# Top-32 attention and a gated feed-forward on one core: one reciprocal for two tiles, low words in PSUM, another queue for the first queries, other slots for the last duos

## The chip, the cores and the metric

The kernel runs on one NeuronCore of one Trainium2 chip. Its engines work side by side, each through its own instructions in order, and meet at semaphores: TensorE (PE, matrix products), VectorE (DVE), ScalarE (ACT), GpSimd (POOL), and SyncE (SP), whose queue issues nearly all transfers. The metric is the device time of one execution in microseconds.

## The reference

The inputs are q, k and v of shape (8, 8, 576, 64) in fp32, and two weight matrices, which the kernel reads as pairs of 32-bit words and turns into fp32 itself.

```
scores = q k^T / sqrt(64)                                # per batch and head, 576 x 576
kth    = the 32nd largest score of each row
attn   = softmax over the scores >= kth (others -1e9), sum + 1e-9
x      = (attn v), heads side by side                    # 4608 x 512
h      = x w_in                                          # 4608 x 2048
out    = (h * clip(h + 3, 0, 6) / 6) w_out               # 4608 x 512
```

## The kernel before, in words

**Tiles.** Two heads form a *pair*, two pairs a *duo*. A duo handles one query tile of 128 rows for two pairs: u is 0 or 1 for the pair, t is 0 or 1 for the head within it. 576 is 4 x 128 + 64, so besides the four full query tiles there is a leftover tile of 64 rows per head; the two heads' leftover rows share one tile of 128 partitions, and such a *leftover duo* has one row tile per pair instead of two. There are 80 duos, 10 for each of 8 batches: 64 full ones and 16 leftover ones. In the last batch the two leftover duos come after query tile 0.

**Selection.** `scores` (PE, then ACT copies out of PSUM) makes the 576 scores of each row. `top` runs four rounds on DVE: MAX8 (L250) finds the eight largest, MATCH_REPLACE8 (L254) takes them out; after four rounds the 32nd largest is known. A full duo takes 16 of the first and 12 of the second.

**Softmax.** For each pair u: `shift` on POOL (L263, L266) forms a bias; `exp` on ACT masks by Prelu (L273), takes Exp with a running sum into `den` (L278), and adds EPS (L283); `inverse` on DVE is the reciprocal of `den` (L287); `weights` on POOL multiplies by it (L297) and splits the words into halves of 16 bits (L306, tile e); `flip` has a DMA of SP's queue transpose these (L312, tile t); `join` puts the halves together again (L318, tile eT), on ACT for u = 0 and on POOL for u = 1. `values` multiplies by v on PE (L338, tile pv), `place` copies the result on ACT into xT, or xr for leftover rows (L348).

**Feed-forward.** When both duos of a query tile are placed, 128 rows of x are complete and a block of feed-forward work is queued: 16 pieces, eight for h (L365, two pieces to one PSUM tile, of which ACT then takes a relu and a copy, L373 and L375, and POOL makes the *gate*, L379 and L380), eight for acc (L385, the product with w_out), at whose end ACT scales (L395) and SP stores (L397).

**Order.** Nothing is scheduled by a compiler: the order of instructions is the order of the program. Duo m owns slots 8m to 8m+7, one DVE round of one pair each. In each slot come, in this order: the round; the parts of any duo that are due there by a table (`usual`, `behind`, `early` for duos 0 and 1, `soon` for the last two); and pieces of feed-forward at a rate that follows how much is queued. In `usual` the second pair's shift stands at slot 8m+7, its Exp at 8m+8, the reciprocals at 8m+9 and 8m+13, the weights at 8m+10 and 8m+14, the transposes at 8m+12 and 8m+16, the joins at 8m+15 and 8m+19, values at 8m+22 (`behind`: 8m+25). The scores of duo m+1 stand at slot 8m+1. A slot is a place in the order, not a time: an engine that has not to wait runs ahead of it, another lags.

**Weights.** 32 chunks of weight words are loaded (st) and converted in the first 150 us, one step per slot: ACT takes the absolute value of the high words (L108, tile a) and scales the low words (L111, tile y); POOL clips a (L109); DVE shifts a (L117) and ORs the sign into y (L118); POOL adds both into the weight (L123). Both a and y come from `gpool` (8 buffers), which the gates' g tiles also use. PSUM has five banks for `ps_big` and three tiles (`ps_w`) for h, acc and pv.

**Start.** SP's queue loads the first pair's keys (three transfers), then its queries (three more), then weights and the other pairs. PE transposes keys and queries (L177), ACT copies them (L179 to L183), PE makes the first scores.

Of the kernel before, what the change touches and what calls it, by code (L numbers as in the profile page):

```python
# [9 lines left out]
ALU = mybir.AluOpType  # L10
F32 = mybir.dt.float32
U32 = mybir.dt.uint32
I32 = mybir.dt.int32
# [16 lines left out]
def kernel(  # L30
# [9 lines left out]
    nc = tc.nc  # L40
    P = nc.NUM_PARTITIONS
    B, H, S, D = q.shape
    DM, FF = moe_w_in.shape
    J = S // P
# [3 lines left out]
    NFC = FF // P  # L48
# [4 lines left out]
    def pool(name, bufs, **kw):  # L53
        return ctx.enter_context(tc.tile_pool(name=name, bufs=bufs, **kw))
# [8 lines left out]
    gpool = pool("g", 8)  # L63
# [3 lines left out]
    ps_w = pool("ps_w", 3, space=PSUM)  # L67
# [25 lines left out]

    WC = 512

    def convert(dst, src):

        st = kqpool.tile([P, 2 * WC], U32, tag="kq", name="st")
        nc.sync.dma_start(st[:], src)
        yield
        words = st[:].rearrange("p (n two) -> p n two", two=2)
        lo, hi = words[:, :, 0], words[:, :, 1]
        a = gpool.tile([P, WC], F32, tag="g", name="a")
        y = gpool.tile([P, WC], F32, tag="g", name="y")
        nc.scalar.activation(a[:], hi.bitcast(F32), AF.Abs)  # L108
        nc.gpsimd.tensor_scalar(a[:], a[:], HI_MOST, HI_LEAST, ALU.min, ALU.max)  # L109

        nc.scalar.activation(y[:], lo, AF.Copy, bias=2.0, scale=2.0**-51)  # L111
        yield

        au, yu = a[:].bitcast(U32), y[:].bitcast(U32)
        nc.vector.tensor_scalar(au, au, 3, None, ALU.logical_shift_left)  # L117
        nc.vector.scalar_tensor_tensor(  # L118
            out=yu, in0=hi, scalar=0x80000000, in1=yu,
            op0=ALU.bitwise_and, op1=ALU.bitwise_or,  # L120
        )
        yield
        nc.gpsimd.tensor_tensor(  # L123
            dst.bitcast(I32), a[:].bitcast(I32), y[:].bitcast(I32), ALU.add
        )

    def weight_chunks():
        win, wout = moe_w_in.bitcast(U32), moe_w_out.bitcast(U32)
        for f in range(0, FF, WC):
            for g in range(NHP):  # L130
                rows = slice(g * P, (g + 1) * P)
                yield w_in[:, g, f : f + WC], win[rows, 2 * f : 2 * (f + WC)]
        for c in range(NFC):
            rows = slice(c * P, (c + 1) * P)
            yield w_out[:, c, :], wout[rows, :]
# [3 lines left out]
    class Pair:  # L139
# [3 lines left out]
            self.b, self.hp = b, hp  # L143
            self.vm, self.vr, self.kr = vms[hp], vrs[hp], krs[b % 2 * NHP + hp]

        def load(self):
            h0 = 2 * self.hp
            t = self.landed = kqpool.tile([P, 2 * J + 1, 2, D], F32, tag="kq", name="landed")
            for i, src in enumerate((k, q)):
                for hh in range(2):  # L150
                    nc.sync.dma_start(
                        t[:, i * J : (i + 1) * J, hh, :],
                        src[self.b, h0 + hh, 0:JP, :].rearrange("(p j) d -> p j d", j=J),
                    )
                nc.sync.dma_start(
                    t[i * R : (i + 1) * R, 2 * J, :, :],
                    src[self.b, h0 : h0 + 2, JP:S, :].rearrange("h s d -> s h d"),
                )
# [26 lines left out]
    class Duo:  # L185
# [82 lines left out]
        def exp(self, u):  # L268

            nt, m = self.nt, self.m[u]  # L270
            for t in range(nt):
                row = self.row(u, t)
                nc.scalar.activation(  # L273
                    row, row, AF.Prelu, bias=m[:, t, TOP_K - 1 : TOP_K], scale=-1.0, alpha=FLAT
                )
            for t in range(nt):
                row = self.row(u, t)
                nc.scalar.activation(  # L278
                    row, row, AF.Exp, bias=self.less[u][:, t : t + 1], scale=-scale / FLAT,
                    accum_out=self.den[:, u, t : t + 1],  # L280
                )
            d = self.den[:, u, 0:nt]
            nc.scalar.activation(d, d, AF.Copy, bias=EPS)  # L283

        def inverse(self, u):
            d = self.den[:, u, 0 : self.nt]
            nc.vector.reciprocal(d, d)  # L287

        def weights(self, u):

# [35 lines left out]
        def values(self, dst):  # L326

            w = R if self.rest else P
            pv = ps_w.tile([P, 512], F32, tag="w", name="pv")
            for u in range(2):  # L330
                pr, eT = self.pairs[u], self.eT[u]
                for c in range(J + 1):
                    for hh in range(2):
                        if self.rest:
                            rhs = eT[:, c if c < J else J + hh, hh * R : (hh + 1) * R]
                        else:
                            rhs = eT[:, c if hh == 0 or c == J else J + 1 + c, :]
                        nc.tensor.matmul(  # L338
                            pv[hh * D : (hh + 1) * D, u * w : (u + 1) * w],
                            pr.vm[:, hh, c, :] if c < J else pr.vr[:, hh, :],  # L340
                            rhs,
                            start=(c == 0),
                            stop=(c == J),
                        )
            self.pv = dst, pv[:, 0 : 2 * w].rearrange("p (u q) -> p u q", u=2)

        def place(self):
            nc.scalar.copy(*self.pv)  # L348
# [55 lines left out]
    duos = []  # L404
    for b in range(B):
        halves = [pairs[b][0:2], pairs[b][2:4]]
        for qt in range(J):
            duos += [Duo(h, qt) for h in halves]


            if qt == (0 if b == B - 1 else J - 1) and not 2 < b < B - 1:
                duos += [Duo(h, J) for h in halves]
            elif 2 < b < B - 1 and qt % 2 == 0:
                duos.append(Duo(halves[qt // 2], J))
    assert J == NHP == 4
    per_batch = 2 * J + 2
    ND = len(duos)
# [65 lines left out]
    chunks = list(weight_chunks())  # L483
    landing, converting, adding = [], [], []

    def land(count=1):

        for _ in range(min(count, len(chunks))):
            c = convert(*chunks.pop(0))
            next(c)  # L490
            landing.append(c)

    def convert_step():


        for c in adding:
            next(c, None)
        adding.clear()
        if len(converting) >= 2 or not landing:
            for c in converting[:1]:  # L500
                next(c)
            adding.extend(converting[:1])
            del converting[:1]
        if landing:
            c = landing.pop(0)
            next(c)
            converting.append(c)
        land()

    def pair_at(m, first):  # L510
# [2 lines left out]
        return pairs[b + 1][at - first] if b + 1 < B and 0 <= at - first < NHP else None  # L513

    first = pairs[0]
    first[0].load()
    land(2)
    first[1].load()
    first[0].transpose()
# [5 lines left out]
    first[1].transpose()  # L525
    duos[0].scores((1,))
    land()

    usual = dict(
        shift0=3, exp0=4, inverse0=9, weights0=10, flip0=12, join0=15,
        shift1=7, exp1=8, inverse1=13, weights1=14, flip1=16, join1=19, values=22, place=23,
    )

    behind = dict(usual, values=25, place=26)
    early = dict(
        shift0=3, exp0=3, inverse0=4, weights0=4, flip0=5, join0=8,
        shift1=7, exp1=7, inverse1=8, weights1=8, flip1=9, join1=12, values=12, place=13,  # L540
    )
    soon = dict(
        shift0=3, exp0=3, inverse0=5, weights0=5, flip0=7, join0=10,
        shift1=7, exp1=7, inverse1=9, weights1=9, flip1=11, join1=14, values=16, place=17,
    )
    queued = {}
    for m in range(ND):
        for part, at in (early if m < 2 else soon if m >= ND - 2 else behind if per_batch <= m < ND - 4 else usual).items():
            queued.setdefault(8 * m + at, []).append((m, part))

    def parts(slot, late=None):

        for m, part in sorted(queued.get(slot, []), key=lambda x: x[1][:-1] != "shift"):
            if late is not None and (part[:-1] in ("inverse", "weights")) != late:
                continue
            if part == "values":
                values(m)
            elif part == "place":
                place(m)
            else:  # L560
                getattr(duos[m], part[:-1])(int(part[-1]))

    due = 0.0
    for m in range(ND + 3):
        u = duos[m] if m < ND else None
        for i in range(8):
            if u:
                u.top(i // 4, i % 4)
            if m < 4:
                parts(8 * m + i, False)  # L570
# [7 lines left out]
            if m < 4:  # L578
                parts(8 * m + i, True)
            else:  # L580
                parts(8 * m + i)
# [54 lines left out]
```

## Time and profile before

| | us |
|---|---|
| median of 5 runs | 1581.66 (1581.34 to 1582.38) |
| the profiled execution | 1582.23 |
| its span in the trace | 1580.4 |
| DVE busy | 1466.7 |
| PE busy | 1460.1 |
| POOL busy | 1143.1 |
| ACT busy | 1095.3 |
| mean granted TensorE clock | 0.961 of full |

DVE and PE are both busy over nine tenths of the span, but not at the same time: the trace shows DVE at work from 11.1 us, in its first selection round at 13.48 us, and at the end of its last at 1492.5 us; PE ends at 1576.7 us. Rows of the timeline give the start and the duration of an instruction (or of several in a row), then engine, line, operation, tile written and tiles read, and in brackets how long the engine stood idle before and what released it. Instructions of one engine overlap by a little, so that what one costs is read from the starts of its neighbours. Waits are listed as: who waited for whom, total, times, longest.

### The profile page before, as it was taken

What the parts mean: (1) busy time and instruction counts of PE and PEld (TensorE: products, weight loads), DVE (VectorE), ACT (ScalarE), POOL (GpSimd) and SP (SyncE); (2) the same over time, 40 slices, a digit from 0 to 9 for tenths busy, and PEclk for the clock granted to TensorE, in tenths of its full rate; (3) what the DMA queues carried; (4) which work ended last, traced back from release to release, by engine and by line L of the source; (5) the groups of instructions that cost most, each with busy time, mean ns of one, the idle gap of its engine ahead of it and who ended that gap; (6) DMA issues with size and microseconds to landing.
All of it is one profiled execution on the core that took longest, in us unless ns stands there. A gap on an engine that the chain in (4) does not pass through costs nothing.

```text
span 1580.4 us, 28787 instructions
## 1 busy us (share of the span) xinstructions
PE 1460.1 (92%) x10272; PEld 1041.7 (66%) x10272; DVE 1466.7 (93%) x3105; ACT 1095.3 (69%) x1865; POOL 1143.1 (72%) x1264
## 2 busy tenths in 40 slices
PE   5256799879999999998999999999999999999899
PEld 3152666567767777676777777776777767677675
DVE  6999999999999999999999999999999999999700
ACT  6675777677776777777776786777766787777521
POOL 4868687777867777767687777777687777767831
PEclk9667899989999999999999999999999999999999
DMA  8652544444444543545244443446344543533400
GB/s 236 159 181 44 114 83 87 88 91 97 79 91 88 97 83 77 104 85 118 57 99 82 99 88 75 93 98 117 56 91 86 100 85 75 105 63 68 83 22 14
DMA packets 450319, 144.49 MB, mean 91 GB/s; under 512 B 433280, under 2 KB 441472, under 8 KB 450176
## 3 DMA queue, kind: packets, MB, share of 16 engines
q1 hardware_dynamic: 450176, 142.65, 43.2%
q8 instruction: 81, 1.33, 0.3%
q14 instruction: 62, 0.51, 0.1%
HBM read 45.09 MB, written 9.44 MB: 35 GB/s over the span
## 4 chain that ended last, share of the span: by engine, by line
DVE 46%; PE 39%; POOL 7%; ACT 3%; issue 3%; DMA 1%; SPq 0%; POOLq 0%; ACTq 0%; DVEq 0%
DVE m L250 24%; DVE wk L254 21%; PE h L365 15%; PE acc L385 14%; PE pv L338 4%; PE big L232 3%; POOL e L306 2%; POOL sc L297 1%; POOL a L109 1%; ACT sc L278 1%; POOL eT L318 1%; ACT eT L318 1%; PE big L177 1%; PE big L215 1%; PE big L226 1%
## 5 line engine op out<-in xcount | busy, mean ns | idle before, releaser
L250 DVE MAX8 m<-wk 128x8 f32<-128x576 f32 x864 | 613.6, 747 | 2.2
L385 PE MATMUL acc<-w_out,g 128*128 128x512 f32 x1152 | 517.8, 601 | 13.6 <-POOL g L380 13.6
L365 PE MATMUL h<-xT,w_in 128*128 128x128 f32 x4096 | 485.9, 279 | 17.3 <-ACT xT L348 17.3
L365 PEld LDWEIGHTS h<-xT,w_in 128*128 128x128 f32 x4096 | 475.4, 195 | 39.6 <-issue 17.9
L254 DVE MATCH_REPLACE8 wk<-m,wk 128x576 f32<-128x576 f32 x576 | 424.0, 743 | 0.0
L385 PEld LDWEIGHTS acc<-w_out,g 128*128 128x128 f32 x1152 | 213.8, 192 | 260.5 <-issue 239.2
L297 POOL TENSOR_SCALAR sc<-sc,den 128x576 f32<-128x576 f32 x288 | 213.2, 750 | 220.9 <-DVE den L287 214.6
L306 POOL COPY e<-sc 128x2304 uint16<-128x2304 uint16 (+1 forms) x192 | 320.0, 1676 | 10.1
L278 ACT ACTIVATE sc<-sc,shift 128x576 f32<-128x576 f32 x288 | 220.3, 769 | 35.3 <-POOL shift L266 32.3
L318 ACT COPY eT<-t 128x2304 uint16<-128x2304 uint16 (+1 forms) x82 | 215.9, 2632 | 36.5 <-DMA t<-e 35.6
L273 ACT ACTIVATE sc<-sc,m 128x576 f32<-128x576 f32 x288 | 209.9, 776 | 40.6 <-DVE m L250 40.4
L338 PE MATMUL pv<-eT,vm 128*64 128x128 f32 (+1 forms) x2560 | 165.0, 274 | 56.2 <-ACT eT L318 45.7
L254 DVE MATCH_REPLACE8 wk<-m,sc 128x576 f32<-128x576 f32 x288 | 212.0, 743 | 0.0
L318 POOL COPY eT<-t 128x2304 uint16<-128x2304 uint16 (+1 forms) x78 | 203.7, 2611 | 7.0 <-DMA t<-e 6.6
L338 PEld LDWEIGHTS pv<-eT,vm 128*64 128x64 f32 x2560 | 136.0, 142 | 107.6 <-ACT eT L318 49.3
L250 DVE MAX8 m<-sc 128x8 f32<-128x576 f32 x288 | 203.5, 744 | 2.0 <-ACT sc L236 2.0
L373 ACT ACTIVATE g<-h,three 128x512 f32<-128x512 f32 x144 | 98.3, 683 | 154.4 <-PE h L365 145.1
L380 POOL TENSOR_TENSOR g<-g,hs 128x512 f32<-128x512 f32 x144 | 184.9, 1284 | 12.2 <-POOL g L379 0.2
L379 POOL TENSOR_SCALAR g<-g 128x512 f32<-128x512 f32 x144 | 89.0, 618 | 75.7 <-ACT g L373 66.1
L233 ACT COPY sc<-big 128x2048 f32<-128x2048 f32 (+1 forms) x65 | 119.2, 1834 | 27.5 <-PE big L232 27.3
L232 PE MATMUL big<-kq 64*128 64x512 f32 x512 | 136.0, 651 | 0.0
L395 ACT ACTIVATE o<-acc 128x512 f32<-128x512 f32 x36 | 21.4, 595 | 111.1 <-PE acc L385 111.1
(47 smaller groups left out, 1115.6 us busy)
## 6 DMA issues: line engine op xcount, KB each, us to landing
landed<-in_k_dram SPq DMA_DIRECT2D x64, 128.0 KB, 2.8
landed<-in_q_dram SPq DMA_DIRECT2D x64, 128.0 KB, 2.9
st<-in_moe_w_in_dram SPq DMA_DIRECT2D x16, 512.0 KB, 4.9
vm<-in_v_dram SPq DMA_DIRECT2D x64, 128.0 KB, 2.3
st<-in_moe_w_out_dram SPq DMA_DIRECT2D x16, 512.0 KB, 6.2
out_dram<-o SPq DMA_DIRECT2D x32, 256.0 KB, 2.4
t<-e SPq DMA_TRANSPOSE x160, 4.6
landed<-in_k_dram SPq DMA_DIRECT2D x32, 32.0 KB, 2.6
```

The costliest lines, as they stand in the source:

```text
L232: nc.tensor.matmul(banks[:, 2 * i + hh, :], pr.qT[d, qs], pr.kT[d, :])
L250: nc.vector.max(self.m[u][:, t, 8 * r : 8 * r + 8], self.cur[t])
L254: nc.vector.match_replace(wk, self.m[u][:, t, 8 * r : 8 * r + 8], self.cur[t], LOWEST)
L273: nc.scalar.activation(row, row, AF.Prelu, bias=m[:, t, TOP_K - 1 : TOP_K], scale=-1.0, alpha=FLAT)
L278: nc.scalar.activation(row, row, AF.Exp, bias=self.less[u][:, t : t + 1], scale=-scale / FLAT, accum_out=self.den[:, u, t : t + 1],)
L297: nc.gpsimd.tensor_scalar(row, row, self.den[:, u, t : t + 1], 1.0, ALU.mult, ALU.mult)
L306: nc.gpsimd.tensor_copy(halves[:, :, to : to + c1 - c0], words)
L318: copy(eT[:, 0 : self.nb, :] .rearrange("p c q -> p (c q)") .bitcast(U16) .rearrange("p (x h) -> p h x", h=2), self.t16[u][:, 0 : 2 * self ...
L338: nc.tensor.matmul(pv[hh * D : (hh + 1) * D, u * w : (u + 1) * w], pr.vm[:, hh, c, :] if c < J else pr.vr[:, hh, :], rhs, start=(c == 0), ...
L365: nc.tensor.matmul(h[:, (f - f0) * P : (f - f0 + 1) * P], w_in[:, i, f * P : (f + 1) * P], xT[:, i, :], start=(i == 0), stop=(i == NHP - 1),)
L380: nc.gpsimd.tensor_tensor(g[:], g[:], hs[:], ALU.mult)
L385: nc.tensor.matmul(acc[:], gs[f // nf][:, f % nf * P : (f % nf + 1) * P], w_out[:, f, :], start=(f == 0), stop=(f == NFC - 1),)
```

## The change

It has four parts.

1. **One reciprocal per duo.** `exp` no longer adds EPS; a new step `settle` does it for one pair or for both, and `inverse` takes the reciprocal for one pair or both. In `usual` both pairs' `settle` stands at slot 8m+8 and one reciprocal at 8m+13. The first pair's weights move from 8m+10 to 8m+13, its transpose from 8m+12 to 8m+15, its join from 8m+15 to 8m+18 (the second pair's transpose and weights stay at 8m+16 and 8m+14, its join at 8m+19). `early` and the new table `last` keep one reciprocal per pair.
2. **Low words in PSUM.** For the first 16 chunks (`early`) ACT writes the scaled low words into a PSUM tile of `ps_w`, and DVE's OR writes its result into a tile of `gpool` taken at that time. The other 16 chunks are as before.
3. **First queries by ACT's queue.** The three transfers of the first pair's queries are issued by ACT instead of SP.
4. **The last duos.** The leftover duos of the last batch come after query tile 1 instead of 0. `soon` now holds for duos 74 to 78, with one reciprocal at 8m+10 and values at 8m+18; duo 79 has `last`, with values at 8m+11; `behind` now ends at duo 71 instead of 75, and duos 72 and 73 have `usual`.

```diff
-    def convert(dst, src):
+    def convert(dst, src, early):
...
-        y = gpool.tile([P, WC], F32, tag="g", name="y")
+        y = (
+            ps_w.tile([P, WC], F32, tag="w", name="yp")
+            if early
+            else gpool.tile([P, WC], F32, tag="g", name="y")
+        )
...
+        ys = gpool.tile([P, WC], F32, tag="g", name="ys") if early else y
...
         nc.vector.scalar_tensor_tensor(
-            out=yu, in0=hi, scalar=0x80000000, in1=yu,
+            out=ys[:].bitcast(U32), in0=hi, scalar=0x80000000, in1=yu,
             op0=ALU.bitwise_and, op1=ALU.bitwise_or,
         )
...
         nc.gpsimd.tensor_tensor(
-            dst.bitcast(I32), a[:].bitcast(I32), y[:].bitcast(I32), ALU.add
+            dst.bitcast(I32), a[:].bitcast(I32), ys[:].bitcast(I32), ALU.add
         )
...
-        def load(self):
+        def load(self, queue=None):
...
-            for i, src in enumerate((k, q)):
+            for i, (src, eng) in enumerate(((k, nc.sync), (q, queue or nc.sync))):
...
-            d = self.den[:, u, 0:nt]
+
+        def inverse(self, us):
+
+            d = self.den[:, us[0] : us[-1] + 1, 0 : self.nt]
+            nc.vector.reciprocal(d, d)
+
+        def settle(self, us):
+            d = self.den[:, us[0] : us[-1] + 1, 0 : self.nt]
             nc.scalar.activation(d, d, AF.Copy, bias=EPS)
-
-        def inverse(self, u):
-            d = self.den[:, u, 0 : self.nt]
-            nc.vector.reciprocal(d, d)
...
-            if qt == (0 if b == B - 1 else J - 1) and not 2 < b < B - 1:
+            if qt == (1 if b == B - 1 else J - 1) and not 2 < b < B - 1:
...
-            c = convert(*chunks.pop(0))
+            c = convert(*chunks.pop(0), early=len(chunks) >= NFC)
...
-    first[0].load()
+    first[0].load(nc.scalar)
...
     usual = dict(
-        shift0=3, exp0=4, inverse0=9, weights0=10, flip0=12, join0=15,
-        shift1=7, exp1=8, inverse1=13, weights1=14, flip1=16, join1=19, values=22, place=23,
+        shift0=3, exp0=4, shift1=7, exp1=8, settle01=8, inverse01=13, weights0=13, weights1=14,
+        flip0=15, flip1=16, join0=18, join1=19, values=22, place=23,
     )
...
     soon = dict(
-        shift0=3, exp0=3, inverse0=5, weights0=5, flip0=7, join0=10,
-        shift1=7, exp1=7, inverse1=9, weights1=9, flip1=11, join1=14, values=16, place=17,
+        shift0=3, exp0=4, shift1=7, exp1=8, settle01=8, inverse01=10, weights0=10, weights1=11,
+        flip0=12, flip1=13, join0=15, join1=16, values=18, place=18,
+    )
+    last = dict(
+        shift0=3, exp0=3, settle0=3, inverse0=5, weights0=5, flip0=7, join0=10,
+        shift1=7, exp1=7, settle1=7, inverse1=8, weights1=8, flip1=9, join1=11, values=11, place=11,
     )
...
-        for part, at in (early if m < 2 else soon if m >= ND - 2 else behind if per_batch <= m < ND - 4 else usual).items():
+        if m < 2:
+            when = early
+        elif m == ND - 1:
+            when = last
+        elif m >= ND - 6:
+            when = soon
+        else:
+            when = behind if per_batch <= m < ND - 8 else usual
+        for part, at in when.items():
```

## The prediction

> **What bounds the kernel now.** I read the page's busy times and slices first, then the waits of DVE and PE, then the timeline at three places: the start, the weight conversion, and the end.
>
> ```profile
> PE 1460.1 (92%) x10272; PEld 1041.7 (66%) x10272; DVE 1466.7 (93%) x3105; ACT 1095.3 (69%) x1865; POOL 1143.1 (72%) x1264
> ...
> PE   5256799879999999998999999999999999999899
> ...
> DVE  6999999999999999999999999999999999999700
> ```
>
> DVE is full from the first to the third-last slice, then stops; PE is thin in the first eight slices and full to the end. So DVE's top-32 rounds set the pace, and PE, which got its work late, drains what is left.
>
> ```profile
> DVE a L117 <- POOL a L109: 13.6, 2, 10.3
> DVE den L287 <- ACT den L283: 10.6, 6, 6.7
> DVE m L250 <- ACT sc L236: 2.0, 2, 1.3
> ```
>
> These are all of DVE's waits but a 0.8 us one for PEq at the start. The 6.7 comes after its last round. In the loop little is left to remove but its instructions.
>
> ```profile
> PE h L365 <- ACT xT L348: 6.0, 2, 3.4
> PE pv L338 <- POOL eT L318: 4.6, 2, 4.4
> PE big L226 <- ACT kr L183: 2.3, 1, 2.3
> ```
>
> PE's waits from 600 us on: it runs out of feed-forward work (h waits for xT) for the last time at 1087 us. Up to there a faster DVE brings PE's work forward one for one; after it PE is never short, and what is gained later counts only through the chain of the last duos. That chain is here:
>
> ```profile
> 1491.87 1.44 ACT L273 ACTIVATE sc<-sc,m 128x576 f32<-128x576 f32 x2 [3.96 <-DVE m L250]
> 1494.12 2.74 POOL L318 COPY eT<-t 128x2304 uint16<-128x2304 uint16 x1
> 1496.91 1.98 PE L338 MATMUL pv<-eT,vm 128*64 128x128 f32 x16 [4.40 <-POOL eT L318]
> 1514.56 1.09 PE L338 MATMUL pv<-eT,vm 128*64 128x128 f32 x16
> 1520.44 14.45 PE L365 MATMUL h<-xT,w_in 128*128 128x128 f32 x128
> ```
>
> DVE's last round ends at 1492.49. PE stands 4.4 us for duo 78's second eT, takes 1.98 where the same group takes 1.09 elsewhere (granted clock 0.75 in 1490 to 1500), and needs until 1576.67: 84.2 us after DVE.
>
> **The change part by part.**
>
> *Reciprocals.* 160 become 83: duos 0, 1 and 79 keep two, 77 save one.
>
> ```profile
> 1484.82 0.74 DVE L254 MATCH_REPLACE8 wk<-m,sc 128x576 f32<-128x576 f32 x1
> ...
> 1485.47 1.41 DVE L250 MAX8 m<-wk 128x8 f32<-128x576 f32 x2
> ...
> 1487.59 0.74 DVE L254 MATCH_REPLACE8 wk<-m,wk 128x576 f32<-128x576 f32 x1
> 1488.25 0.15 DVE L287 RECIPROCAL den<-den 128x2 f32<-128x2 f32 x1
> 1488.32 1.40 DVE L250 MAX8 m<-wk 128x8 f32<-128x576 f32 x2
> ```
>
> The row says 155 ns, but instructions overlap: replace to MAX8 is 0.65 without and 0.73 with it; the chain of waits books 0.07. So 77 x 0.07 = 5.4 us (6.2 at 0.08), not 11.9. Four elements instead of two cost nothing: 128x1 and 128x2 rows both lie in 142 to 167 ns. The EPS step (0.20 us on ACT) also goes 77 times, on an engine 69% busy: nothing.
>
> What moves: POOL's weights of tile 0 go from slot 10 to 13, so both tiles stand on POOL back to back behind one reciprocal: 1.47 + 2.10, twice, 7.1 us instead of 3.6. Behind them in POOL's order are the gates and the next duo's second shift, due 4.9 us after the reciprocal. The idle that POOL has today between the second reciprocal and that shift is mostly 0.5 us, so the shift slips by 3.0 to 3.6 us in almost every duo, and ACT's Exp with it. In its favour, the join of tile 0 (2.8 us, sometimes waiting for its transpose) leaves its place ahead of that Exp in ACT's order for one behind it. The reciprocal comes 14.5 us after the shift's due time in a full duo: covered. PE's cover is three PSUM tiles; its h groups today find the tile of two groups before free by 0.7 us at least, of three before by far more. SP issues the same transposes, one slot apart; outputs and loads behind them are not due for slots. I take +1 us (end: +22, below).
>
> *Low words in PSUM.* The OR of the first 16 chunks reads one input from PSUM and no second one from SBUF.
>
> ```profile
> 71.93 1.79 DVE L117 TENSOR_SCALAR a<-a 128x512 uint32<-128x512 uint32 x1
> 73.64 1.75 DVE L118 SCALAR_TENSOR_TENSOR y<-st,y 128x512 uint32<-128x512 uint32 x1
> ...
> 81.09 0.41 DVE L117 TENSOR_SCALAR a<-a 128x512 uint32<-128x512 uint32 x1
> 81.42 0.68 DVE L118 SCALAR_TENSOR_TENSOR y<-st,y 128x512 uint32<-128x512 uint32 x1
> ```
>
> It takes 0.68 alone and 1.09 or 1.75 beside POOL's work on the same tiles; over the first 16 chunks 4.5 us above 0.68. No row shows DVE reading PSUM. Ends: ACT's PSUM copy of the same size, 0.58, would give 6.0; if nothing is freed, 0. I take 2.9: the unheld row for most, some holding coming back at L117, which keeps its 5.3 us of excess. [...] PSUM has three tiles for this; chunk s needs chunk s-3's OR done, which today is so 3 us or more before. The second tile that the change takes from the g pool is taken later than today's, so ACT waits for g buffers no longer than now.
>
> *First queries on ACT's queue.* Three issues on SP, 2.82 to 4.77, go; ACT issues them before its table load (1.28 us, then about 2.7 to 4.0, with the first copy at 7.90).
>
> ```profile
> 6.53 0.93 PEld L177 LDWEIGHTS big<-ident,landed 128*128 128x128 f32 x5 [1.39 <-DMA landed<-in_q_dram]
> ...
> 7.90 1.01 ACT L179 COPY kq<-big 128x1024 f32<-128x1024 f32 x1 [5.90 <-PE big L177]
> ...
> 13.48 1.42 DVE L250 MAX8 m<-sc 128x8 f32<-128x576 f32 x2 [1.32 <-ACT sc L236]
> ```
>
> The chain from the queries to DVE's first round is unbroken, so what they land earlier, DVE starts earlier: 2.1 us at most (the issue times), nothing if the transfers share the engines. DMA share is 0.54 to 0.74 there, so most fits: 1.5. [...]
>
> *A gap that goes along.* At 133.7 DVE idles 3.30 us for POOL's clip; ACT waits 9.12 us for a g tile behind weights of tile 0 (125.62). Those weights now stand two rounds later. 0 to 3.3; I take 2.2.
>
> *Last six duos.* Pv 78 and 79 stand at slots 642 and 643, after the leftover block's h; in PE's order 20 matmuls of acc (8.6 us) and two blocks (56.1) follow, where 8 (3.6) and two blocks follow today. PE, never short, would reach pv 79 at today's 1576.7, less 10.5 (the gains below, by 1087), less 7.0 (today's standing at 1492 and the slow clock after it), less 67.0 (pv, acc, two blocks): 1492.2, which is E+11.7 if E is DVE's unstalled end in the sum below. But ACT's relu of the leftover block's first h, ready 18.2 us of PE work earlier (E-6.5), stands before duo 79's first Exp: with 1.2 + 3.5 its den comes at E-1.8, 3.0 late for the reciprocal (two slots before the end), so DVE ends at E+3.0. Then POOL in its order: gate, shift (to E+4.2), join 78 (2.8); ACT's Exp to 7.9; weights 3.6 (to 11.8), two gates (3.8); the transpose, 4.6, lands at 16.4, join to 19.2. Then half a pv 1.2, acc 8.6, blocks 56.1: E+85.1, and 1.5 for the clock, which also today follows PE's idling. So 86.6 against 84.2: the shorter chains gain nothing, because more is put behind them. Ends: 78.7 without the stall, 89 if two more gates (3.8) slip in ahead.
>
> **Sum.** 1492.5 - 5.4 - 2.9 - 1.5 - 2.2 = 1480.5 (E); + 86.6 + 1.0 = 1568.1; + 3.7 from the last matmul to the span's end as today = 1571.8; + 1.8 outside the span (1582.23 against 1580.4) = 1573.6. The profiled execution lies 0.57 above the median, so **1573**.
>
> **Rivals.**
> *The burst on POOL reaches DVE (slower).* Eight duos next to a leftover duo have their second den ready less than 3.6 us before the reciprocal (8, 18, 28, 41, 46, 61, 66, 72); slipped by their 3.0 to 3.6 they give 22.4 us of new waits: 1573 + 21 = 1594. For: four of them stand at 0.03 us now. Against: at 61 and 72 ACT, not POOL, was late, with the join before the Exp, which is moved. It decides from 12 us on.
> *PE hides it.* PE is 92% busy; if its last starvation isn't DVE's doing, little of DVE's gain arrives and the tail gives back 2.4: 1580 to 1582. Against: h waits for xT at 317, 730 and 1087.
> *The tail is free.* If the relu doesn't hold duo 79, 78.7 instead of 86.6: 1565. For: PE's lag behind its slot is a difference of large numbers.
> *Start and low words do nothing:* 1573 + 4.4 = 1577.4, inside the forecast's own range.
>
> **How the numbers follow.** Forecast 0.62 (own range 1567 to 1578), tail free 0.14, hidden 0.09, slower 0.15. The range 1563 to 1582 holds all but the slower case and a thin end. A measurement here tells 0.2% (3.2 us) from nothing: faster 0.76, same 0.09, slower 0.15.
>
> **What would show it.** 83 reciprocals; OR rows of the first 16 chunks near 0.7 us throughout; first MAX8 near 12.0; no idle at 133; DVE's last round near 1483.5, and PE's end 84 after it, with PE idle before duo 79's second half. Wrong if DVE den waits rise above 10 us inside the loop, or PE waits for PSUM tiles or gates.

## The result: slower by 3.3 us

| | before | after |
|---|---|---|
| median, us | 1581.17 (1579.76 to 1582.47, 48 runs) | 1584.45 (1581.86 to 1587.03, 28 runs) |
| ratio, 95% interval | | 1.002 (1.0015 to 1.0026) |
| profiled execution, us | 1582.23 | 1583.52 |
| end of DVE's last round, us | 1492.49 | 1490.54 |
| end of PE, us | 1576.65 | 1577.90 |
| DVE's waits for den inside the loop, us | 3.47 | 13.30 |

1573 was predicted, within 1563 to 1582; the result lies outside, on the slow side. The two profiled executions differ by 1.3 us, less than the medians; the changed kernel's runs spread more widely (5.2 us against 2.7). A ratio, here and below, is the time over that of the kernel before on the same chip; the interval reaches 0.9 us to either side here, and 1.3 to 2.2 us in the experiments.

### The profile after

Line numbers from here on are those of the changed kernel. The page's busy times and slices:

```profile
PE 1458.8 (92%) x10272; PEld 1039.8 (66%) x10272; DVE 1458.3 (92%) x3028; ACT 1079.9 (68%) x1788; POOL 1134.4 (72%) x1264
...
PE   5266898889999999998999999999999999999989
...
DVE  6999999999999999999999999999999999989600
```

DVE has 77 instructions fewer and is busy 8.4 us less (1466.7 before), yet it ends only 2 us sooner. The one slice of PE below 9 near the end was the third-last before and is the second-last now. DVE's waits (who for whom, total, times, longest) show what took its gain:

```profile
DVE den L293 <- ACT den L297: 19.5, 8, 5.6
DVE a L123 <- POOL a L114: 9.9, 1, 9.9
DVE m L257 <- ACT sc L243: 1.7, 1, 1.7
```

The wait for POOL's clip at 133.7 us is gone (13.6 in two waits before, now one), and the waits for den have nearly doubled, 10.6 to 19.5. One of them, 5.6, lies after the last round and holds nothing up; 0.63 lies at the start; 13.3 are in the loop.

PE's waits from 600 us on:

```profile
PE pv L348 <- POOL eT L328: 6.7, 1, 6.7
PE h L375 <- ACT xT L358: 5.0, 2, 3.7
PE big L233 <- ACT kr L190: 3.4, 1, 3.4
PE pv L348 <- ACT eT L328: 2.7, 2, 1.5
```

One stand of 6.7 us has taken the place of the 4.4 before. The timeline of all engines at the end shows where:

```profile
1492.88 1.43 ACT L280 ACTIVATE sc<-sc,m 128x576 f32<-128x576 f32 x2
...
1501.59 1.09 PE L348 MATMUL pv<-eT,vm 128*64 128x128 f32 x16 [1.23 <-ACT eT L328]
...
1506.80 2.73 POOL L328 COPY eT<-t 128x2304 uint16<-128x2304 uint16 x1 [2.18 <-DMA t<-e]
...
1509.59 1.97 PE L348 MATMUL pv<-eT,vm 128*64 128x128 f32 x16 [6.69 <-POOL eT L328]
```

PE is at the last duo's products at 1500.4 us, and waits 1.23 us for ACT's join of the first half and 6.69 for POOL's of the second, which itself stood for the transpose. Before, PE came to these products at 1514.56, after the joins were done. PE's own timeline tells what it does only afterwards:

```profile
1511.92 9.93 PE L395 MATMUL acc<-w_out,g 128*128 128x512 f32 x20
1521.68 14.45 PE L375 MATMUL h<-xT,w_in 128*128 128x128 f32 x128
```

The 20 matmuls of acc at 1511.92 needed nothing that the last duo makes. The start and the first conversions, in the timelines of all engines and of DVE:

```profile
5.63 1.78 PEld L184 LDWEIGHTS big<-ident,landed 128*128 128x128 f32 x9 [5.63 <-issue]
7.85 1.01 ACT L186 COPY kq<-big 128x1024 f32<-128x1024 f32 x1 [3.80 <-PE big L184]
...
13.43 0.76 DVE L257 MAX8 m<-sc 128x8 f32<-128x576 f32 x1 [1.69 <-ACT sc L243]
```

```profile
60.95 0.41 DVE L123 TENSOR_SCALAR a<-a 128x512 uint32<-128x512 uint32 x1
61.28 0.68 DVE L124 SCALAR_TENSOR_TENSOR ys<-st,yp 128x512 uint32<-128x512 uint32 x1
```

```profile
71.47 1.48 DVE L123 TENSOR_SCALAR a<-a 128x512 uint32<-128x512 uint32 x1
72.87 1.09 DVE L124 SCALAR_TENSOR_TENSOR y<-st,y 128x512 uint32<-128x512 uint32 x1
```

All nine transposes begin together at 5.63, the first copy of kq is at 7.85 (7.90 before) and the first MAX8 at 13.43 (13.48). The OR of an early chunk reads yp in PSUM and takes 0.68; at 71 us the first of the late chunks, with its low words in SBUF, still takes 1.09.

### The profile page after: what moved, and what is told of

Same layout as the page of the kernel before. It is cut to its first block, busy times and chain, and to the rows that moved or that the text cites. A ratio compares the mean times of both kernels' runs of the same rounds, so it can differ in the third digit from the quotient of the medians.

```text
span 1581.7 us, 28611 instructions
## 1 busy us (share of the span) xinstructions
PE 1458.8 (92%) x10272; PEld 1039.8 (66%) x10272; DVE 1458.3 (92%) x3028; ACT 1079.9 (68%) x1788; POOL 1134.4 (72%) x1264
## 4 chain that ended last, share of the span: by engine, by line
DVE 60%; PE 19%; POOL 10%; issue 4%; ACT 3%; DMA 2%; SPq 1%; POOLq 0%
DVE m L257 31%; DVE wk L261 27%; PE h L375 8%; PE acc L395 8%; POOL e L316 3%; POOL sc L307 2%; PE pv L348 2%; DMA t<-e 2%; POOL eT L328 2%; PE big L239 1%; POOL g L390 1%; ACT sc L285 1%; DVE a L123 1%; POOL g L389 1%; DVE y L124 1%
## 5 line engine op out<-in xcount | busy, mean ns | idle before, releaser
L240 ACT COPY sc<-big 128x2048 f32<-128x2048 f32 (+1 forms) x65 | 119.3, 1835 | 27.2 <-PE big L239 27.1
L270 POOL TENSOR_TENSOR shift<-m 128x2 f32<-128x2 f32 (+1 forms) x160 | 33.2, 208 | 121.3 <-DVE m L257 121.2
```

## The experiments

Two theories stood at first. *The burst:* with one reciprocal both tiles' weights stand back to back on POOL, the next shift and so the next den come late, and DVE waits. *The tail:* the new order and tables of the last duos cost at the end. Medians below stand beside the kernel before on the same chip.

### Each part alone, or taken out

**One reciprocal alone.** The changed kernel with the other three parts undone:

```
-            c = convert(*chunks.pop(0), early=len(chunks) >= NFC)
+            c = convert(*chunks.pop(0), early=False)
-    first[0].load(nc.scalar)
+    first[0].load()
...
     (order, soon and the choice of tables as before; soon with settle0 and settle1)
```

> The kernel before with one reciprocal per duo alone (usual and behind; the last two duos keep two). Theory 'burst': both tiles' weights back to back on POOL hold the next second shift, and at the leftover duos the denominators come late: DVE's den waits inside the loop 9 to 16 us (before 3.5, after 13), which eats the 5.5 us of reciprocals and the 3.3 us gap at 133 us; time 1579 to 1585. Rival 'tail': the loss lies in the last duos alone, den waits cost nothing that counts; then this is 5 to 9 us faster than before, 1572 to 1576.

1583.22 us (1580.29 to 1585.79) against 1580.9, ratio 1.0014 (1.0005 to 1.0023). Den waits in the loop 13.86 us, DVE's end 4.3 us later than before, PE's 81.9 us after it. DVE's waits for den, the start and the end included:

```profile
DVE den L293 <- ACT den L297: 21.1, 10, 6.8
```

The part that removes instructions from the busiest engine makes the kernel 2.3 us slower by itself (0.8 to 3.6 by the interval).

**Everything but the one reciprocal.**

```
-        shift0=3, exp0=4, shift1=7, exp1=8, settle01=8, inverse01=13, weights0=13, weights1=14,
-        flip0=15, flip1=16, join0=18, join1=19, values=22, place=23,
+        shift0=3, exp0=4, settle0=4, inverse0=9, weights0=10, flip0=12, join0=15,
+        shift1=7, exp1=8, settle1=8, inverse1=13, weights1=14, flip1=16, join1=19, values=22, place=23,
```

> The changed kernel with two reciprocals and the old slots of weights, transposes and joins in usual and behind (duos 74 to 79 as changed). Burst: ACT's waits for POOL's shift fall from 171 us to about 30, den waits inside the loop from 13 to under 6 us, although the reciprocals cost 5 us again; time 1576 to 1581, that is 3 to 8 below the changed kernel. Tail: 1584 to 1590, since the tail is as changed and the reciprocals are back.

1582.81 us (1581.19 to 1585.31), ratio 1.0012 (1.0003 to 1.0021). Den waits are down to 3.8 us and DVE ends 4.7 us sooner than before, but PE ends 88.2 us after it.

```profile
DVE den L293 <- ACT den L297: 10.3, 4, 6.5
```

The time met neither forecast: it is above the 1576 to 1581 of the burst and below the 1584 to 1590 of the tail. It is 1.6 us under the changed kernel, and the two intervals overlap, so it is the wait that shows the burst here and not the time. The burst is real, and not the whole.

**The old tail.** The changed kernel with order and tables of the last duos as before:

```
-            if qt == (1 if b == B - 1 else J - 1) and not 2 < b < B - 1:
+            if qt == (0 if b == B - 1 else J - 1) and not 2 < b < B - 1:
...
-        elif m == ND - 1:
-            when = last
-        elif m >= ND - 6:
+        elif m >= ND - 2:
             when = soon
```

> The changed kernel with the last duos as before (leftover duos after query tile 0, old tables, the last two duos with two reciprocals). Burst: den waits inside the loop 8 to 13 us still, PE's end 84 us after DVE's last round instead of 87; time 1579 to 1583. Tail: 1571 to 1575, because the 5.5 of reciprocals, 3 of low words and 3 of the gap come through.

1579.46 us (1576.59 to 1582.34), ratio 0.9994 (0.9986 to 1.0003): 5.0 us under the changed kernel. The tail, from the end of DVE's last round to PE's end, is 84.5 us (87.4 in the changed kernel), den waits still 13.7. Each theory holds a part, and neither all.

**Weights of the second tile later,** an attempt to break up the burst inside the changed kernel:

```
-... weights0=13, weights1=14, flip0=15, flip1=16, join0=18, join1=19, values=22, place=23,
+... weights0=13, weights1=16, flip0=15, flip1=18, join0=18, join1=21, values=23, place=24,
```

> The changed kernel, one reciprocal per duo, but the second tile's weights three slots after the first's (slot 16 instead of 14, behind the next duo's second shift), its transpose at 18 and join at 21. Burst: the shift is on time again, ACT's waits for it fall from 171 to under 60 us, den waits inside the loop under 5 us, DVE's last round ends 8 to 10 us earlier than in the changed kernel (about 1481); time 1574 to 1578. Tail: within 2 us of the changed kernel's 1584. Against both: weights of the second tile come later, so scores of the duo after next may wait for their buffer, and PE then shows waits for copies of scores.

1598.77 us, ratio 1.0115 (1.0101 to 1.0129). Den waits rose to 18.4 us in the loop, and DVE also waited 8.1 us for ACT's copies of the scores (1.7 in the changed kernel, at the start in both). ACT's waits for the shift fell from 171 to 106 us, where under 60 was expected, and in their place ACT's copies of the scores (L240) waited 67.6 us, 39 times, for POOL's e, which they did not wait for in the changed kernel: sc tiles stay taken until the second weights are done. A later slot does not spread the burst; it hands the lateness on.

**Low words and queue alone** (two reciprocals, old tail), and **low words alone:**

```
     usual: two reciprocals, as above; order, soon and the choice of tables as before
     (second kernel also)
-    first[0].load(nc.scalar)
+    first[0].load()
```

> Two reciprocals per duo, the old order and the old tables at the end: only the low words in PSUM and the first queries on ACT's queue are left of the change. Theory (the last duos cost about 4 us, the burst on POOL about 10 us of waits for den, the low words give 4 us): DVE's last round ends 4.7 us before that of the kernel before, as it did with two reciprocals and the new end (1487.8 us), den waits within 4 us, and PE's end comes 84 to 85 us after it, so the time is 1577 us, 4 us under the kernel before. Rival (the end is not what costs; the low words' gain is lost further on whatever the end): tail 88 us again, and the time is that of the kernel before or above, 1581 to 1583 us.

> The low words of the first chunks in PSUM alone: two reciprocals, old order and tables, and the first queries on SP's queue as before. Theory (the queue of the first queries is worth nothing, since the keys land later by as much as the queries land sooner): first MAX8 within 0.2 us of 13.5 us, time within 1 us of the 1576.5 us that both together gave. Rival (it was worth the predicted 1.5 us): 1578 us.

1576.49 us (1575.96 to 1577.27), ratio 0.997 (0.996 to 0.9981), and 1575.87 us (1575.27 to 1578.95), ratio 0.9974 (0.9965 to 0.9983). The low words give 4.9 us by the medians (1580.77 - 1575.87) and 4.1 by the ratio; the queue adds nothing. The first MAX8 stands at 13.50 with it and at 13.15 without; in all the traces it stands at 13.31 to 13.63 with the second queue (eleven kernels) and at 13.15 to 13.52 without (three).

**The tail's two halves.** Short tables with the old order, and new order with the old tables:

```
  first kernel
-            if qt == (1 if b == B - 1 else J - 1) and not 2 < b < B - 1:
+            if qt == (0 if b == B - 1 else J - 1) and not 2 < b < B - 1:
  second kernel: that line as changed; soon and the choice of tables as before
```

> The changed kernel with the leftover rows of the last batch back at their old place, after its first two duos; the shorter tables of the last six duos stay. Theory (the later place of the leftover rows puts their feed-forward block behind DVE's end, and this is what the end of the change costs): PE ends 82 to 85 us after DVE's last round, and the time is 1579 us, that of the kernel with the old order and old tables, or up to 2 us less. Rival (the short tables cost: PE's products, ACT's copies and joins of six duos meet ACT's Exp of the last ones): tail 87 to 88 us as in the changed kernel, 1583 to 1585 us.

> The changed kernel with the old tables at the end, and the new place of the last batch's leftover rows alone (after its second two duos). Theory (the later place is what costs): PE ends 87 to 90 us after DVE's last round, more than today's 87.4 us, since the old tables put place and values later still, and the time is 1584 to 1587 us. Rival (the short tables cost): tail 84 to 85 us, and 1579 to 1580 us as with the old order and old tables.

1584.32 us (1581.94 to 1585.56) with the short tables, 1579.72 us (1576.56 to 1584.49) with the new order. Here my own theory fell: I had laid the 5 us on the later place of the leftover rows. The order is free (1579.46 without it); the tables are the 5 us. In the profiled executions of these two kernels (1582.63 and 1580.09) the difference is only 2.5, so the traces below show part of it.

### What the tables do

In every one of these traces PE waits for xT for the last time between 1083 and 1097 us. From there to the end it has the same 3398 matmuls to do, and pauses that I sum from its idle times:

| kernel | last wait for xT ends | busy, 3398 matmuls | of it lost to the clock | pauses | PE ends |
|---|---|---|---|---|---|
| before | 1090.81 | 481.20 | 4.20 | 4.64 | 1576.65 |
| after | 1088.42 | 480.09 | 2.26 | 9.39 | 1577.90 |
| old tail | 1089.39 | 480.08 | 2.81 | 6.73 | 1576.20 |
| short tables, old order | 1087.88 | 480.26 | 2.28 | 8.90 | 1577.04 |
| new order, old tables | 1089.73 | 479.08 | 1.62 | 5.69 | 1574.50 |
| low words and queue | 1087.24 | 478.77 | 1.66 | 4.66 | 1570.67 |
| two reciprocals, new tail | 1085.58 | 482.02 | 4.12 | 8.34 | 1575.93 |
| low words alone | 1087.55 | 481.17 | 4.18 | 4.65 | 1573.37 |

Wait, busy time and pauses add up to the last column, to 0.01. In the first six rows the end of the last wait follows DVE to 0.2 us: at its 817th MAX8 (1073 us) DVE was ahead of before by 2.55, 1.58, 3.12, 1.25 and 3.55 us, and the last wait for xT ended sooner by 2.39, 1.42, 2.93, 1.08 and 3.57. In the last two rows it follows less closely: ahead by 3.63 and 4.26, sooner by 5.23 and 3.26. "Lost to the clock" is half of the busy time in which the granted clock stood at 0.50; without it the 3398 matmuls take 477.0 to 478.0 us in every row. The pauses are what the end of the order makes. With the short tables (after, short tables, two reciprocals) they are 8.3 to 9.4 us, and 7.7 to 7.9 of them stand in front of the two halves of the last duo's products (1.23 or 1.24, and 6.45 to 6.69). So one number of the table of the last duo was moved, and with it eight matmuls of w_out (in the kernel's order; the profile counts each as two) from behind those products to ahead of them:

```
-        shift1=7, exp1=7, settle1=7, inverse1=8, weights1=8, flip1=9, join1=11, values=11, place=11,
+        shift1=7, exp1=7, settle1=7, inverse1=8, weights1=8, flip1=9, join1=11, values=15, place=15,
```

> The changed kernel with one edit: values and place of the last duo at slot 15 instead of 11 of its table. Theory (PE reaches the last products too early): the pauses of 1.23 and 6.69 us at 1500 to 1510 us shrink to about 1 us in all, the matmuls behind them fall from 68.3 to 61 us, and the time is 1577 to 1578.5 us, 6 to 7 us under the changed kernel. Rival (the end is set by the backlog that the new tables leave, not by this place in the order): no more than 2 us gained, 1582.5 us or more.

1575.18 us (1573.71 to 1575.74), ratio 0.9962 (0.995 to 0.9975): 9.3 us under the changed kernel by one slot number, more than the 6 to 7 expected. PE's timeline at the end:

```profile
1504.43 5.42 PE L395 MATMUL acc<-w_out,g 128*128 128x512 f32 x12 [0.53 <-POOL g L390]
1509.78 1.09 PE L348 MATMUL pv<-eT,vm 128*64 128x128 f32 x16
...
1510.92 1.04 PE L348 MATMUL pv<-eT,vm 128*64 128x128 f32 x16
...
1512.12 1.98 PE L395 MATMUL acc<-w_out,g 128*128 128x512 f32 x4
1513.94 14.45 PE L375 MATMUL h<-xT,w_in 128*128 128x128 f32 x128
```

No wait for a join is left at the end; PE's pauses are 2.38 us (9.39 before the edit), and the next block begins at 1513.94 instead of 1521.68. The clock shows a second gain. First the changed kernel, then this one (window, its length, PE's busy time and matmuls, granted clock, DMA share, GB/s):

```profile
1500.00:1510.00 10.00, 2.08 (x25) 0.69 0.32 61
1510.00:1520.00 10.00, 10.00 (x37) 0.79 0.00 0
```

```profile
1500.00:1510.00 10.00, 9.47 (x30) 1.00 0.32 61
1510.00:1520.00 10.00, 10.00 (x99) 1.00 0.12 27
```

In the window in which the pause ends the granted clock is 0.69, and 0.79 in the next; without the pause it is 1.00 in both, and the same 3398 matmuls take 478.17 us instead of 480.09. In the profiles, 7.0 of pauses and 1.9 of clock, less 1.2 because the last wait for xT ended at 1089.60 and not 1088.42, make 7.7 of the 7.8 us between the executions (1583.52 and 1575.74). DVE ends at 1492.36 here, within 0.2 us of the kernel before, and PE 6.5 us sooner: the place of the products in PE's order sets this end as much as DVE does. With this one place moved, the changed kernel is also 4.3 us under the one with the old tail (1579.46): it is not the shorter tables as such that cost, but where they put the last products.

### Where the burst costs

At 590 us, in the changed kernel's timeline of all engines:

```profile
583.58 1.49 POOL L307 TENSOR_SCALAR sc<-sc,den 128x576 f32<-128x576 f32 x2
...
585.14 2.10 POOL L316 COPY e<-sc 128x2304 uint16<-128x2304 uint16 x1
...
587.22 1.47 POOL L307 TENSOR_SCALAR sc<-sc,den 128x576 f32<-128x576 f32 x2
...
588.74 2.10 POOL L316 COPY e<-sc 128x2304 uint16<-128x2304 uint16 x1
...
590.93 0.61 POOL L389 TENSOR_SCALAR g<-g 128x512 f32<-128x512 f32 x1
...
592.86 0.19 POOL L270 TENSOR_TENSOR shift<-m 128x1 f32<-128x1 f32 x1
...
593.40 0.77 ACT L285 ACTIVATE sc<-sc,shift 128x576 f32<-128x576 f32 x1 [5.69 <-POOL shift L273]
...
594.53 0.17 DVE L293 RECIPROCAL den<-den 128x2 f32<-128x2 f32 x1 [4.37 <-ACT den L297]
```

The two pairs of weights and copies of duo 27 fill POOL from 583.58 to 590.84 (588.74 + 2.10), a gate follows, and the shift for the second tile of duo 28 comes at 592.86. ACT's Exp waits 5.69 us for it, and DVE's reciprocal, due at 590.16 (594.53 - 4.37), 4.37 us for the den. The kernel before, at the same duos:

```profile
589.83 1.47 POOL L297 TENSOR_SCALAR sc<-sc,den 128x576 f32<-128x576 f32 x2
591.37 2.10 POOL L306 COPY e<-sc 128x2304 uint16<-128x2304 uint16 x1
...
595.48 0.19 POOL L263 TENSOR_TENSOR shift<-m 128x1 f32<-128x1 f32 x1
...
597.50 0.15 DVE L287 RECIPROCAL den<-den 128x1 f32<-128x1 f32 x1
```

There only the second tile's weights are left by then. POOL is through them at 593.47, 4.0 us before the reciprocal of duo 28's second tile at 597.50, which finds its den ready; in the changed kernel it is through them 0.7 us after the reciprocal is due. Duo 28 is leftover rows: with eight MAX8 rows instead of a full duo's sixteen, the four rounds of one of its pairs take 5.61 us where those of a full pair take 9.70 (588.72 to 594.33 and 599.94 to 609.64 in the kernel before), so the next den is due sooner after the burst. The next kernel therefore keeps two reciprocals wherever one of the two following duos is leftover rows (28 of 80 duos), with the old tail; its sequel keeps them also from duo 72 on:

```
+            when = dict(usual) if any(d.rest for d in duos[m + 1 : m + 3]) else dict(merged)
  second kernel
+            close = m >= ND - 8 or any(d.rest for d in duos[m + 1 : m + 3])
+            when = dict(usual) if close else dict(merged)
```

Here usual is the table with two reciprocals, merged that with one.

> Old order and tables at the end; one reciprocal for a duo only where neither of the next two duos is one of a batch's leftover rows, two reciprocals (the schedule of the kernel before) for the others. Theory (the burst on POOL reaches DVE only where short leftover duos leave POOL no slack): den waits fall from 13.7 us, as they are with one reciprocal everywhere, to 3 to 5 us, the idle 3.3 us near 133 us stays away, some 50 reciprocals at 0.05 us are saved, so DVE's last round ends 9 to 10 us before that of the kernel before, 1482.5 to 1484 us; with a tail of 84.5 us the time is 1572 us. Rival (the waits move to whichever duo has the next thin slack): den waits of 9 us or more at other duos, DVE's end within 4 us of 1489, and 1577 us or more, no better than two reciprocals everywhere.

> The mixed kernel (old order and tables at the end, one reciprocal only where neither of the next two duos is leftover rows) with two reciprocals also from duo 72 on. Theory (the mixed kernel's 4 us at the front of DVE were lost to den waits of duos 74 to 77 and to the pause of 3.1 us in front of PE's products at 1479 us with the dropped clock behind it): PE runs dry for the last time until 1084 us as in the mixed kernel, no pause before 1485 us is above 0.5 us, its 3398 matmuls from there take 479 to 480 us and the pauses 4.7 us, PE ends at 1567 to 1569 us and the time is 1573 us, 3 to 4 us under that with two reciprocals everywhere. Rival (what DVE gains before 1090 us is made up by PE in any case): 1576 us, as with two reciprocals everywhere.

1576.71 us (1576.22 to 1578.94), ratio 0.9975 (0.9965 to 0.9985), and 1574.74 us (1573.59 to 1575.49), ratio 0.996 (0.9948 to 0.9973). In the first, DVE is 7.0 us ahead at 1430 us (5.2 with two reciprocals everywhere). The waits at duos 8, 28, 41 and 46 are gone (7.9 us in the old tail's trace), so there the burst was their cause. But those at duos 18 and 61 grew, from 0.93 to 2.99 and from none to 1.78, though these duos keep two reciprocals; 1.53 stands at duo 72; and den waits of 1.56 and 2.00 us at 1462 and 1473, at duos 77 and 78, take half of the lead. In all 9.9 us are left in the loop where 3 to 5 were expected, and the time is the rival's: no better than two reciprocals everywhere. PE pays with a pause at the end and with the clock behind it. Its PE timeline:

```profile
1482.51 1.35 PE L348 MATMUL pv<-eT,vm 128*64 128x128 f32 x16 [3.08 <-POOL eT L328]
...
1484.86 6.29 PE L375 MATMUL h<-xT,w_in 128*128 128x128 f32 x32 [0.57 <-ACT hs L385]
```

Those 32 matmuls of h take 3.84 us elsewhere, and 6.29 here, where the granted clock is 0.66. The second kernel has neither wait; den waits fall to 5.7 us (2.60 of them at 411 us, 1.48 at 1173) and PE's last wait for xT ends at 1083.15. It was expected at 1573 and stands 1.75 us under the 1576.49 of two reciprocals everywhere, about half of what was expected, and the two intervals overlap. DVE is 7.3 us ahead at 1073 us instead of 3.55, but part of that comes back to PE as matmul time (480.18 instead of 478.77), because more of it is lost to the clock (3.16 instead of 1.66). The waits that are left at 411 and 1173 (duos 18 and 61) are not POOL's: their shifts were done at 409.1 and 1165.0, but ahead of their Exp ACT stood 2.2 us for a transpose, joined (from 408.01 and 1167.71) and took an h tile, so that the Exp's first step began at 411.90 and 1171.41. The faster DVE met the next engine that was late.

**Both cures in the changed kernel:** mixed reciprocals and the last duo's products at slot 15.

```
-            when = behind if per_batch <= m < ND - 8 else usual
+            close = any(d.rest for d in duos[m + 1 : m + 3])
+            when = dict(usual) if close else dict(merged)
+            if per_batch <= m < ND - 8:
+                when.update(values=25, place=26)
...
+        ... join1=11, values=15, place=15,
```

> The changed kernel with the mixed reciprocals (two for a duo where one of the next two is leftover rows) and, in the table of the last duo, values and place 4 slots later (15 instead of 11), so that 8 more matmuls of w_out stand ahead of the last duo's products. Theory (the end costs 5 us because PE reaches the last duo's products 7.9 us before ACT and POOL have joined them): pauses of PE after 1480 us sum to 2 to 3 us instead of 9.4, PE's last starvation ends near 1084 us, PE ends at 1566 to 1569 us, time 1571 to 1573 us. Rival (the pause only moves: PE waits elsewhere for the same work, as the products are late by DVE's end): PE's pauses stay at 8 us or more and the time is 1577 us or more.

1570.95 us (1569.66 to 1571.56), ratio 0.9935 (0.9922 to 0.9949), 9.8 us under the kernel before. All that PE stands at the end:

```profile
1493.82 1.09 PE L348 MATMUL pv<-eT,vm 128*64 128x128 f32 x16 [0.51 <-POOL eT L328]
...
1499.45 5.42 PE L395 MATMUL acc<-w_out,g 128*128 128x512 f32 x12 [0.69 <-POOL g L390]
```

1084.28 + 479.69 + 1.20 = 1565.17, PE's end. It is the fastest kernel here, and 4.2 us under the one with slot 15 alone (1575.18; the intervals of the ratios do not meet). Its loop still has 8.4 us of den waits, the longest 3.45 us at 411.6 and 2.98 at 1399.2. No run has two reciprocals everywhere together with slot 15, so what the remaining merges are worth in this kernel is not shown.

## Why the prediction was wrong

The four parts, from the runs: one reciprocal costs 2.3 us (alone) or 3.0 (1579.46 with it against 1576.49 without, old tail), the low words give 4.1 to 4.9, the queue 0, the last duos cost 5.0. The sum is 2.4 to 3.9, and 3.3 was measured. A part's price depends on the others: with the new tail one reciprocal costs 1.6, and with two reciprocals the last duos cost 6.3 (1582.81 against 1576.49).

- **What bounds.** Right. DVE's lead at 1073 us reached PE's last wait for xT within 0.2 us in five of the seven traces of the table, and in the changed kernel's trace PE is short after that wait only in front of the last duos' products.
- **Reciprocals, -5.4.** 83 are there. Between 144 and 222 us, four duos without a den wait, DVE's lead grew from 7.59 to 7.81 us: 0.055 per reciprocal saved, 4.2 for 77. A little over-sized.
- **"I take +1 us" for the burst: the step that failed.** The waits in the loop rose from 3.5 to 13.3 us; without the one at 1485, which belongs to the last duos, to 12.1, so 8.6 us in place of 1. Not all of that is the burst: 4.13 of it is duo 74's, where the new table has the one reciprocal at slot 10, and 2.76 of those remain with two reciprocals in the other duos. Alone or with the old tail the waits rose by 10.4 and 10.3 us. The text saw that the shift slips in almost every duo and named eight duos with too little slack, priced them at 22.4, and then took a value next to the other end. Of the eight, 8, 28, 46 and 66 did wait (1.68, 4.37, 1.70 and 0.19); 18, 41 and 61 did not; 72 has other neighbours in the new order. That ACT's order was better after the move was no protection, since ACT itself waits for the shift. The mark "wrong if DVE den waits rise above 10 us inside the loop" was met. Half of the rival's price would have been the better guess.
- **Low words, -2.9.** Better than said: the ORs of the first 16 chunks lie 0.08 us under 0.68 each in sum, where they lay 4.44 above, and L117's excess over 0.41 each fell a little too, from 5.3 to 4.5, instead of taking some back. That the OR takes 0.68 "alone" was read too narrowly: it does so beside POOL's clip as well (see the last section). DVE's lead at 78 us without part 1 is 3.8 to 4.0.
- **First queries, -1.5: failed.** What the queries gain the keys lose: the first four transposes no longer start ahead of the rest, and all nine stand at 5.63, where the first four began at 4.43 before. The first MAX8 moved by 0.05 us. That "most fits" under a DMA share of 0.54 to 0.74 did not come true.
- **The gap at 133.7, -2.2.** Larger: 3.30 became 0.08. It goes with part 1: with two reciprocals and the rest of the change it is still there, 3.31 at 129.7.
- **Last six duos, 86.6 from DVE's unstalled end E: mis-sized by 2.0, and its effect on the whole read too mildly.** The relu did hold the den of duo 79's first half, by 1.23 us and not 3.0; E was 1489.3. The last join was done 20.2 us after E instead of 19.2, acc took 9.9 instead of 8.6 at the dropped clock, and PE ended 88.6 after E. The reciprocal of duo 74, moved to slot 10, was put at nothing and waited. The place where PE would stand was predicted, and that more is put behind it. That the 7.9 us there could be had back by one slot number was not seen.

In the terms of the sum: E came 8.8 us later than the 1480.5 predicted, the tail was 2.0 longer, and the 1.0 for the burst has to come off again: 9.8 of the 9.9 us between 1573.6 and the profiled 1583.52. This is an account in the prediction's form; that form is itself weak, since the time from DVE's last round to PE's end was no constant but ran from 77.8 us (slot 15) to 88.6 (short tables, old order). Of the rivals, the burst was the right mechanism at two to three times its price; "PE hides it" was not what happened; "the tail is free" was the opposite of the runs.

Part of DVE's gain came back as a longer time of the same 3398 matmuls, 478.2 to 482.9 us over all fourteen traces. The granted clock accounts for it: less what was lost to it, they take 477.0 to 478.2 us in each. Not all of that loss follows the pauses at the end. In the kernel before, 3.4 us at a clock of 0.50 come at 1092, behind the last wait for xT (3.37 us, to 1090.81); behind a wait of the same 3.37 us in low words and queue (to 1087.24) there are none, and the clock stands at 1.00 from 1050 to 1130.

What stays open is when PE's standing is followed by such a stretch, and how long it is.

## What to carry to other kernels

Merging two small instructions on the busiest engine also merges what hangs on them: here the saved 0.055 us per duo was lost where 7.3 us in one piece on POOL stood ahead of the next duo's shift. Price such a merge at the duos with the least slack, and keep it away from them; that took 4.2 us off the changed kernel with slot 15, and nothing clear of the intervals with the old tail. At the end of a kernel look for the engine that drains the backlog, and place the last dependent work in its order where its inputs are ready, with independent work ahead of it: shortening the chain by slots was worth nothing here, where PE came 7.9 us too early.

## What the runs showed of the hardware

- DVE's OR with one input in PSUM took 0.67 to 0.68 us in all 16 early chunks. With both inputs in SBUF it took 0.68 too where POOL ran only its clip, which reads one tile (at 48.14, 51.92, 64.78 and 68.55 before); the six of the first 16 that took 1.09 or 1.75 all lay beside a POOL TENSOR_TENSOR, which reads two inputs. From PSUM, four that lay wholly beside such an instruction (at 24.63, 38.92, 54.23 and 69.53 after) still took 0.68.
- Two queues instead of one for keys and queries did not bring the first round forward (13.43 against 13.48). The three query issues, on SP from 2.82 to 4.77 before, stood on ACT from 0.72; the nine transposes began together at 5.63, where four had begun at 4.43 and five at 6.53.
- At four pauses of PE near the end, of 3.08 to 6.69 us, the granted clock of the 10 us window in which the pause ended was 0.66 to 0.83 (0.69 in the changed kernel, 0.75 in the one before, 0.83 with low words and queue, 0.66 in the first mixed one). These pauses cost more than themselves: in the changed kernel 16 matmuls of pv took 1.97 us behind the one of 6.69, and 1.09 at 1501.59, ahead of it. How much more differs between runs: the same pause of 4.40 us came with 6.8 us at a clock of 0.50 in the kernel before (from 1495.1), and with 3.4 us in low words and queue (from 1491.6).
